# Batches 2 to 7 of a fused Fourier and ELU kernel in a schedule of 48 steps

## The chip, the core and the metric

The kernel runs on one core of a Trainium2 chip. The metric is the time of one execution on the device in microseconds (us). The kernel before takes 1938.01 us, the median of three runs (1937.81 to 1938.64). A measurement of this kernel can tell a difference of about 0.2% from none.

## The reference

Each of 8 batches of 3008 rows and 256 channels gets a two-dimensional Fourier transform, of which the real part is kept; the 24064 rows then go through two matrix products with an ELU between them.

```python
def _attn_ref(x):                     # x: (8, 3008, 256), float32
    X = np.fft.fft(x, axis=1)
    X = np.fft.fft(X, axis=2)
    return X.real.astype(np.float32)

def _moe_ref(x, w_in, w_out):         # x: (24064, 256), d_ff = 2048
    h = x @ w_in
    g = np.where(h > 0.0, h, np.exp(np.minimum(h, 0.0)) - 1.0)
    return (g @ w_out).astype(np.float32)
```

## The kernel before

**Folding.** The transform over channels is folded into the first weight matrix (Wc for cosines, Ws for sines), so what is left of the front is a transform over rows. Rows k and 3008-k of the result share their cosine and sine parts, P and Q: one gets P+Q, the other P-Q. So the kernel works on half of the frequencies, 1504 columns a batch, of which the first 752 are the even and the last 752 the odd frequencies (`kodd` 0 and 1).

**The main loop.** The 8 x 1504 columns are cut into 47 output tiles of 256. A tile takes 8 steps, one for each pair of feature blocks of 128, so there are 376 steps, and a batch is 47 steps long. In a step, with S as its number:

- `mm_P` starts the PSUM bank H with Wc times the cosine ring Rr, `mm_Q` adds Ws times the sine ring Ir (`first_mm`).
- VectorE adds the one cosine row that has no place in 128 rows (`even_part`, E, L1179) between the two, and after `mm_Q` makes the other half (`h_minus`, L1193).
- ScalarE makes Relu and Exp of both (`below_*`, `exp_*`), and in the next step VectorE finishes the ELU (`g_plus`, `g_minus`, L1209).
- GpSimd makes four sums of blocks of G (`sum_1` to `sum_4`), with which seven products do the work of eight (`mm_X1`, `mm_X2`, `mm_X3`, after Winograd); they add up in the banks pA to pD over the 8 steps of a tile.

A matmul in the code is two TensorE instructions in the trace, so a step has 22. When a tile is done, VectorE combines the banks (`comb_1`, `comb_2` in the step with number 1 modulo 8, `comb_22`, `comb_3` at 2), transposes (`turn_u` at 3, `turn_v` at 4) and SyncE stores it.

**The row transforms.** The rings Rr, Ir and Rb hold 2048 columns, so a batch's transforms are made while the batch before is in the loop. Batches 0 and 1 are made by the class `Dft`. For batches 2 to 7 the rows are loaded in quarters (`load_quarter`: four tiles xl0 to xl3, `far` 0 and then 1; each of the two loads has two plain DMAs and two gathers on GpSimd's queue). Then:

- `mirror_sum` on GpSimd adds mirrored rows, `half_sum` on VectorE adds or subtracts halves (two instructions of 256 elements), `channel_fold` on GpSimd and `channel_edge` on ScalarE fold the channels.
- `quarter_pairs` makes the last sums: for even frequencies on GpSimd, for odd ones on VectorE, as pairs of scalar_tensor_tensor with a table of tangents ("twisted pairs", L756).
- The class `Quarter` does the transform of each of four kinds (real or imaginary part `ri`, even or odd `kodd`), each in two halves. `mms` are eight TensorE instructions into a bank H; `copy`, `unfold`, `copy_odd` and `unfold_odd` turn banks into runs of columns, and `plus` and `minus` ("join") write both halves of the ring.

**The order.** It is written out by hand. Every piece of work is entered with a due time, `at(step * T + offset, function)` with T = 4.8, and emitted in order of these times; engine instructions made through `pin` keep that order on their engine, while plain SyncE DMAs aren't pinned. So each engine runs one fixed queue, and what is late in it makes all behind it late. In a step VectorE's queue has `even_part` at 0.9, the unfolding and joining at 1.0, `g_plus` at 2.2, `g_minus` at 2.9, `h_minus` at 3.55, and at 4.2 or 4.25 the tile's combining, the transposes, `half_sum` and the twisted pairs. GpSimd's folds stand at 1.3, between `sum_4` and the next `sum_1` (2.91). A transform's matmuls stand at 4.75, ahead of the next step.

For batch b the times are given from s0 = 47(b-1): the first loads at s0-12, the second ones at s0+7, the transforms at s0+28, s0+32, s0+36 and s0+42. As 47 is no multiple of 8, these lie in another place of the output tile for every batch. The function `pause` moves `half_sum` and the twisted pairs out of places 1, 3 and 4. `safe` is the first step at which a column of the ring may be written again.

Of the kernel before, what the change touches and what calls it, by code (L numbers as in the profile page):

```python
# [31 lines left out]
QW = (1133, 1134)  # L32
GW = 7 * TW
PERIOD = 4.8


def _dft_consts():
# [124 lines left out]
def kernel(  # L162
# [112 lines left out]
    def load_quarter(b, j, far):  # L275

        L = spool.tile([128, 6 * ND], FP, tag=f"xl{j}", bufs=1, name=f"xq{j}")
        state["L", j, far] = L = L[:, 0 : 4 * ND]
        back = j in (1, 2)
        base = (0, SEQ, HALF, HALF)[j]  # L280
        if back != far:
            n = 94 if far else 96
            c = 3 if far else 5 if j == 1 and b == NB - 1 else 4
            pin(
                nc.gpsimd.indirect_dma_start(
                    out=L[0:n],
                    out_offset=None,
                    in_=xflat,
                    in_offset=bass.IndirectOffsetOnAxis(
                        ap=ix[0:n, c : c + 1].bitcast(U32), axis=0  # L290
                    ),
                    element_offset=(b * SEQ + (HALF if j in (1, 3) else 0)) * ND,
                )
            )
            return
        row = base - 751 if far else base
        for p, q in ((0, 80), (80, 94)) if far else ((0, 96),):
            nc.sync.dma_start(out=L[p:q], in_=xrows(b, row + 8 * p, 8, q - p, 4))
# [430 lines left out]
                act(L[0:1, i * ND : i * ND + ND], L[0:1, i * ND + ND : i * ND + 2 * ND])  # L729
        act(L[0:1, 3 * ND :], state["L", 0, 0][0:1, 0:ND])  # L730

    def quarter_pairs(ri, kodd, m):
# [3 lines left out]
        if m == 1 + kodd:  # L736
            state["pairs"] = spool.tile([128, 384], FP, tag="side", bufs=2, name="pairs")
            state["Q", ri, kodd] = {0: near[0:95, 0:128], 4: slot(4)}
        new, parts = state["pairs"], state["Q", ri, kodd]
        for k in (m,) if kodd else (1, 2, 3):  # L740
            parts["u", k], parts["v", k] = new[0:94, 128 * k - 128 : 128 * k], slot(8 - k)
        if not kodd:
            a, b = (
                t[0:94, 128:512].rearrange("p (m d) -> p m d", d=128)
                for t in (near, far)
            )
            o = new[0:94].rearrange("p (m d) -> p m d", d=128)
            if m == 1:
                gtt(o, a, b[:, ::-1], ALU.add)
            else:  # L750
                gtt(b[:, ::-1], a, b[:, ::-1], ALU.subtract)
            return
        for i, o in ((0, parts["u", m]), (1, parts["v", m])):
            c = 4 * (0, 2, 1)[m - 1] + 2 * ri + i
            pin(
                nc.vector.scalar_tensor_tensor(  # L756
                    out=o, in0=parts["v", m], scalar=twist_tab[0:94, c : c + 1],
                    in1=slot(m), op0=ALU.mult, op1=ALU.add,
                )
            )  # L760
# [59 lines left out]
    class Dft:  # L820
# [18 lines left out]
            act(self.anti[0:M, 0:h], self.even[0:M, h : 2 * h])  # L839

        def unfold(self):
            self.es = spool.tile([128, NE], FP, tag="bs", bufs=3, name="bs")
            unfold(self.es, self.even, self.anti, self.M, self.n, vtt)

        def copy_odd(self):
# [43 lines left out]
    class Quarter(Dft):  # L889
# [50 lines left out]

        def unfold(self):
            M, ri, kodd = self.M, self.ri, self.kodd
            na, nc_ = (94, 188) if kodd else (95, 189)
            n = NO if kodd else NE
            self.es = es = spool.tile([128, NE], FP, tag="bs", bufs=3, name="bs")
            ab = spool.tile([128, 2 * NH], FP, tag="ab", bufs=1, name="ab")
            a, b = self.even[0:M, 0:na], self.near[0:M, 0:na]
            vtt(ab[0:M, 0:na], a, b, ALU.add)
            p, q = (b, a) if ri else (a, b)
            vtt(ab[0:M, steps_of(nc_ - 1, 94, -1)], p[:, 0:94], q[:, 0:94], ALU.subtract)  # L950
            if kodd:
                c = ab[:, NH : 2 * NH]
                self.spread(c, self.even[:, 94:189], self.near[:, 94:189], 94)
                runs = ((0, 1, 188, 188, c),)
            else:
                runs = (
                    (0, 2, 95, 94, self.even[:, 190:285]),
                    (1, 2, 94, 94, self.even[:, 285:379]),
                )
            for h, step, up, down, c in runs:  # L960
                i = steps_of(h, up, step)
                vtt(es[0:M, i], ab[0:M, i], c[0:M, 0:up], ALU.add)
                p, q = ab[0:M, steps_of(h, down, step)], c[0:M, 0:down]
# [9 lines left out]

        def unfold_odd(self):
            if self.kodd:
                t = spool.tile([128, NE], FP, tag="bs", bufs=3, name="od")
                self.spread(t, self.odd, self.far, 188)
                self.odd = t

# [119 lines left out]
    def ext_unfold(kodd, tt, rows=NB):  # L1099
        n = NO if kodd else NE  # L1100
        h = (n + 1) // 2
        even = state["side", 0]
        a = spool.tile([128, NE], FP, tag="bs", bufs=3, name="bs")
        unfold(a, even, even[:, h : 2 * h], rows, n, tt)
        state["es"] = a[0:rows]

# [621 lines left out]
    def at_half(step, d, par, col):  # L1728
# [6 lines left out]

        at(t + 4.75, run)
        if par:
            at(t + T + 0.9, lambda: d().copy_odd())
            at(t + T + 1.0, lambda: d().unfold_odd())
# [6 lines left out]
    def at_dft(step, gap, b, ri, kodd, stat):  # L1746
        box = []

        def d():
            if not box:  # L1750
                box.append((Quarter if b > 1 else Dft)(ri, b, kodd, stat()))
            return box[0]

        at_half(step, d, 0, 0)
# [28 lines left out]
    at(35 * T + 4.76, lambda: ext_side(3))  # L1783
    at(36 * T + 0.2, lambda: ext_unfold(1, vtt))
    at(36 * T + 1.5, lambda: ext_rows(1, vtt))
    at(34 * T + 4.3, quarter_table)
    at(34 * T, lambda: nc.sync.dma_start(out=twist_tab[0:96], in_=QT_dr.ap()))
    for n in range(4):
        at(
# [22 lines left out]
    for kodd, step in ((0, 37), (1, 40)):  # L1812
        at(step * T + 1.0, lambda kodd=kodd: spread_ext(1, kodd))

    for b in range(2, NB):
        s0 = (b - 1) * steps_b
        def pause(step):
            while step % 8 in (1, 3, 4):
                step += 1
            return step  # L1820

        for far, start in ((0, s0 - 12), (1, s0 + 7)):
            for j, n in ((0, 0), (1, 0), (3, 1), (2, 1)):
                gather = (j in (1, 2)) != far
                at(
                    (start + n) * T + (1.3 if gather else 0.2),
                    lambda b=b, j=j, far=far: load_quarter(b, j, far),
                )
            if not far:
                at((start + 2) * T + 3.0, lambda b=b: quarter_row(b))  # L1830
            work, sums, step = start + 3, {}, 0
            for n in range(8):
                h, m, j = n // 4, n // 2, (0, 3)[n % 2]
                at(work * T + 1.3, lambda j=j, far=far, m=m: mirror_sum(j, far, m))
                if n % 4 == 3:
                    step = max(work, step)
                    for kodd in range(2):
                        step = sums[h, kodd] = pause(step + 1)
                        at(
                            step * T + 4.25,  # L1840
                            lambda kodd=kodd, far=far, h=h: half_sum(kodd, far, h),
                        )
                work += 1
            for n in range(8):
                h, kodd, ri = n // 4, n // 2 % 2, n % 2
                work = max(work, sums[h, kodd] + 1)
                key = (ri, kodd, far, h)
                at(work * T + 1.3, lambda key=key: channel_fold(*key))
                if h and not ri:
                    at(  # L1850
                        work * T + 4.0,
                        lambda kodd=kodd, far=far: channel_edge(kodd, far),
                    )
                work += 1
            assert far or work <= s0 + 7
        for n in range(4):
            ri, m = divmod(n, 2)
            at((work + n) * T + 1.3, lambda ri=ri, m=m: quarter_pairs(ri, 0, 1 + m))
        step = 0
        for n in range(6):  # L1860
            ri, m = divmod(n, 3)
            step = pause(max(step + 1, s0 + (31, 35)[ri]))
            at(
                step * T + 4.25,
                lambda ri=ri, m=(2, 1, 3)[m]: quarter_pairs(ri, 1, m),
            )
        for ri, kodd, step in ((0, 0, 28), (1, 0, 32), (0, 1, 36), (1, 1, 42)):
            at_dft(
                s0 + step, 2, b, ri, kodd, lambda ri=ri, kodd=kodd: state["Q", ri, kodd]
            )  # L1870
# [52 lines left out]
```

## Time and profile before

| what | value |
|---|---|
| median of three runs | 1938.01 us |
| profiled execution | 1939.31 us |
| its span, first to last instruction | 1937.5 us |
| granted TensorE clock, mean | 0.999 |
| matmul instructions | 9008 |
| VectorE, ScalarE, GpSimd instructions | 2714, 1710, 1843 |
| DMA | 71.88 MB, mean 37 GB/s |

The profile comes from one execution, which took 1939.31 us; the span leaves out 1.8 us around it. Engines are named PE (TensorE's matmuls), PEld (its weight loads), DVE (VectorE), ACT (ScalarE), POOL (GpSimd) and SP (SyncE, which issues DMAs). In rows of the timeline, start and duration come first, then engine, source line, operation, what is written and read, shape and count, and in brackets the idle time before it with what ended it. Nearly all matmuls have line L536, GpSimd's sums L545 and VectorE's sums L542, since helpers record them; they are told apart by tiles. H<-Rr is `mm_P`, H<-Ir is `mm_Q`, H<-QM is a transform of batches 2 to 7. xq is a tile of loaded rows, bs and ab are tiles of the unfolding, od that of the odd half, e and o the tiles of the channel folds.

### The profile page before, as it was taken

To read this page: it belongs to the slowest core of one execution; us is meant where nothing else is said; L and a number is where in the kernel's file an instruction comes from. 1 tells how busy PE (TensorE), PEld (TensorE's weight loads), DVE (VectorE), ACT (ScalarE), POOL (GpSimd) and SP (SyncE) were. 2 spreads that over 40 slices of the span, in tenths; PEclk is the share of its full clock that TensorE was granted. 3 is DMA by queue.
4 is the path that set the end of the run, shared out by engine and by line. 5 is a ranking of instruction groups with operands and counts; after the bars stand their busy time and mean duration, and the time that the engine had idled before them with its cause. 6 is when DMAs were issued, how large, how long until landed. Compare 5 with 4: busy or idle time off the path is not lost.

```text
span 1937.5 us, 27618 instructions
## 1 busy us (share of the span) xinstructions
PE 1922.8 (99%) x9008; PEld 1651.0 (85%) x9008; DVE 1421.3 (73%) x2714; ACT 873.8 (45%) x1710; POOL 1352.6 (70%) x1843
## 2 busy tenths in 40 slices
PE   9999999999999999999999999999999999999999
PEld 6788788888888888888888888888888888888887
DVE  8876666777867687676776768777687777767666
ACT  5644444444444444444444444444444444444443
POOL 4788767775677767776677766777667775556555
PEclk9999999999999999999999999999999999999999
DMA  8145212011011120210111101011011110100101
GB/s 334 44 35 35 60 31 56 19 31 41 11 46 28 21 46 11 50 31 13 42 21 43 33 10 43 20 44 42 15 30 28 36 21 16 17 12 12 23 11 23
DMA packets 271072, 71.88 MB, mean 37 GB/s; under 512 B 256814, under 2 KB 257730, under 8 KB 270928
## 3 DMA queue, kind: packets, MB, share of 16 engines
q1 hardware_dynamic: 257296, 57.34, 14.8%
q0 software_dynamic: 11456, 12.52, 2.1%
q8 instruction: 71, 1.16, 0.2%
q14 instruction: 73, 0.60, 0.1%
q10 hardware_dynamic: 2176, 0.26, 0.1%
HBM read 45.20 MB, written 24.80 MB: 36 GB/s over the span
## 4 chain that ended last, share of the span: by engine, by line
PE 89%; DVE 6%; POOL 2%; DMA 1%; issue 1%; SPq 0%; ACT 0%; DVEq 0%; POOLq 0%
PE H L536 35%; PE pC L536 15%; PE pD L536 15%; PE pB L536 15%; PE pA L536 7%; DVE E L1179 2%; DVE G L1209 1%; PE M L536 1%; POOL G L545 1%; DMA out_dram<-ot 1%; POOL WT L545 1%; DVE G L1193 1%; SPq L1410 0%; DVE v L542 0%; DVE bs L542 0%
## 5 line engine op out<-in xcount | busy, mean ns | idle before, releaser
L545 POOL TENSOR_TENSOR G<-G 128x256 f32<-128x256 f32 x1440 | 1041.2, 732 | 528.6 <-DVE G L1209 405.4
L548 ACT ACTIVATE G<-H 128x512 f32<-128x512 f32 x376 | 224.5, 597 | 938.0 <-DVE G L1193 933.3
L1179 DVE SCALAR_TENSOR_TENSOR E<-Rb,wex,H 128x256 f32<-128x256 f32 x752 | 327.2, 476 | 420.1 <-PE H L536 412.9
L536 PE MATMUL H<-Ir,Ws 128*128 128x256 f32 x1504 | 390.8, 382 | 5.5 <-DVE E L1179 5.3
L536 PE MATMUL H<-Rr,Wc 128*128 128x256 f32 x1504 | 387.8, 380 | 0.8 <-DVE Ir L542 0.8
L536 PE MATMUL pC<-G,WT 128*128 128x256 f32 x1440 | 370.4, 380 | 0.0
L536 PEld LDWEIGHTS H<-Ir,Ws 128*128 128x128 f32 x1504 | 276.4, 189 | 62.9 <-DVE E L1179 19.9
L536 PEld LDWEIGHTS H<-Rr,Wc 128*128 128x128 f32 x1504 | 282.1, 190 | 43.7 <-issue 2.2
L536 PEld LDWEIGHTS pC<-G,WT 128*128 128x128 f32 x1440 | 274.2, 190 | 37.5
L1193 DVE SCALAR_TENSOR_TENSOR G<-E,H 128x512 f32<-128x512 f32 x376 | 256.7, 683 | 42.3 <-POOL G L545 10.3
L1209 DVE SCALAR_TENSOR_TENSOR G<-G,H 128x512 f32<-128x512 f32 x376 | 255.5, 679 | 33.0 <-ACT G L548 32.8
L1209 DVE SCALAR_TENSOR_TENSOR G<-M,G 128x512 f32<-128x512 f32 x376 | 256.4, 682 | 0.4 <-ACT M L548 0.4
L548 ACT ACTIVATE G<-G 128x512 f32<-128x512 f32 x376 | 233.3, 621 | 0.0
L536 PE MATMUL pB<-G,w 128*128 128x256 f32 x784 | 229.4, 379 | 0.0
L536 PE MATMUL pD<-G,w 128*128 128x256 f32 x784 | 229.2, 379 | 0.0
L536 PE MATMUL pA<-G,w 128*128 128x256 f32 x784 | 229.2, 379 | 0.0
L548 ACT ACTIVATE M<-G 128x512 f32<-128x512 f32 x376 | 224.2, 596 | 3.1 <-DVE G L1193 3.1
L548 ACT ACTIVATE M<-M 128x512 f32<-128x512 f32 x376 | 221.1, 588 | 0.1
L536 PE MATMUL pB<-G,WT 128*128 128x256 f32 x720 | 216.1, 382 | 2.8 <-POOL G L545 2.5
L536 PE MATMUL pD<-G,WT 128*128 128x256 f32 x720 | 215.0, 380 | 0.4 <-DVE v L542 0.4
L536 PEld LDWEIGHTS pD<-G,w 128*128 128x128 f32 x784 | 149.1, 190 | 20.3
L536 PEld LDWEIGHTS pA<-G,w 128*128 128x128 f32 x784 | 148.9, 190 | 20.5
(178 smaller groups left out, 1528.7 us busy)
## 6 DMA issues: line engine op xcount, KB each, us to landing
out_dram<-ot SPq DMA_DIRECT2D x496, 32.0 KB
xq<-in_x_dram SPq DMA_DIRECT2D x12, 384.0 KB
out_dram<-ot SPq DMA_DIRECT2D x256, 2.0 KB
xq<-in_x_dram SPq DMA_DIRECT2D x12, 320.0 KB
Rb<-r SPq DMA_DIRECT2D x10, 376.0 KB
raw<-in_moe_w_in_dram SPq DMA_DIRECT2D x7, 512.0 KB
MC<-dft_mats SPq DMA_DIRECT2D x3, 943.5 KB
xl<-in_x_dram SPq DMA_DIRECT2D x4, 512.0 KB
```

The source lines that it names most:

```text
L536: nc.tensor.matmul(out_, lhsT=lhsT, rhs=rhs, start=start, stop=stop, skip_group_check=True)
L545: pin(nc.gpsimd.tensor_tensor(out=o, in0=a, in1=b, op=op))
L548: pin(nc.scalar.activation(out=o, in_=i, func=func, **kw))
L1179: nc.vector.scalar_tensor_tensor(out=S.E[:, c], in0=Rb[:, cols(i)], scalar=wex[:, f : f + 1], in1=S.H[:, c], op0=ALU.mult, op1=ALU.add,)
L1193: nc.vector.scalar_tensor_tensor(out=two(S.G[:, 0:512])[:, :, ::-1], in0=two(S.E), scalar=2.0, in1=two(S.H), op0=ALU.mult, op1=ALU.subtract,)
L1209: nc.vector.scalar_tensor_tensor(out=o, in0=e, scalar=-1.0, in1=h, op0=ALU.add, op1=ALU.max)
```

## The change

- Batches 2 to 7 get a table of steps counted from r0 = 48b - 70, so that each piece stands at the same place in an output tile for all batches. Loads, sums, folds, pairs, transforms and joins all get new steps. For batch 2, whose r0 is 26, the first load moves from step 35 to 28; for batch 7 it moves from 270 to 268. The loop over batches remains 47 steps a batch.
- `Quarter` is entered by a function of its own, `at_quarter`. For odd frequencies `unfold` is parted: its last two instructions become `finish`, entered at offset 4.26 of a step of its own, and `plus` and `minus` move from the step of `unfold_odd` to offset 4.25 of a later step.
- The small tile "ab" goes; its work is done in the last third of the tile xl0 (`state["rest"]`), which the quarter loads leave free. Twisted pairs are written into the free last third of the fold tiles e and o instead of tiles "side".
- The tag "bs" has four buffers instead of three. The state of the pairs is kept for each batch.
- `quarter_table` (four small instructions on GpSimd) moves from step 34 to 27.

The core of the diff:

```diff
+BS = 4
...
         L = spool.tile([128, 6 * ND], FP, tag=f"xl{j}", bufs=1, name=f"xq{j}")
+        if j == 0:
+            state["rest"] = L[:, 4 * ND :]
...
+        new = (near, near, far)[m - 1][0:94, (512, 640, 512)[m - 1] :]
+        parts["u", m], parts["v", m] = new[:, 0:128], slot(8 - m)
...
         def unfold(self):
             M, ri, kodd = self.M, self.ri, self.kodd
-            na, nc_ = (94, 188) if kodd else (95, 189)
-            n = NO if kodd else NE
-            self.es = es = spool.tile([128, NE], FP, tag="bs", bufs=3, name="bs")
-            ab = spool.tile([128, 2 * NH], FP, tag="ab", bufs=1, name="ab")
+            na, top = (94, 187) if kodd else (95, 188)
+            self.ab = ab = state["rest"]
             a, b = self.even[0:M, 0:na], self.near[0:M, 0:na]
             vtt(ab[0:M, 0:na], a, b, ALU.add)
             p, q = (b, a) if ri else (a, b)
-            vtt(ab[0:M, steps_of(nc_ - 1, 94, -1)], p[:, 0:94], q[:, 0:94], ALU.subtract)
+            vtt(ab[0:M, steps_of(top, 94, -1)], p[:, 0:94], q[:, 0:94], ALU.subtract)
             if kodd:
-                c = ab[:, NH : 2 * NH]
+                c = ab[:, ND : ND + NH]
                 self.spread(c, self.even[:, 94:189], self.near[:, 94:189], 94)
-                runs = ((0, 1, 188, 188, c),)
+            else:
+                self.finish()
+
+        def finish(self):
+            M, ri, kodd, ab = self.M, self.ri, self.kodd, self.ab
+            n = NO if kodd else NE
+            self.es = es = spool.tile([128, NE], FP, tag="bs", bufs=BS, name="bs")
+            if kodd:
+                runs = ((0, 1, 188, 188, ab[:, ND : ND + NH]),)
             else:
...
-    at(34 * T + 4.3, quarter_table)
+    at(27 * T + 4.3, quarter_table)
...
+    def at_quarter(step, b, ri, kodd, finish, join):
...
+        at(step * T + 4.75, lambda: half(0))
+        at((step + 1) * T + 0.9, lambda: d().copy())
+        at((step + 1) * T + 1.0, lambda: d().unfold())
+        at((step + 2) * T + 4.75, lambda: half(1))
+        if kodd:
+            at(finish * T + 4.26, lambda: d().finish())
+            at((step + 3) * T + 0.9, lambda: d().copy_odd())
+            at((step + 3) * T + 1.0, lambda: d().unfold_odd())
+        assert join + 1 >= safe(b * HALF + (kodd + 1) * RUN)
+        t = join * T + (4.25 if kodd else 1.01)
+        at(t, lambda: d().plus())
+        at(t + 0.001, lambda: d().minus())
...
+        r0 = 48 * b - 70
+
+        def rel(step, dt, fn, *key):
+            at((r0 + step) * T + dt, lambda: fn(*key))
+
+        for far, rows in (
+            (0, ((0, 2, 0.2), (1, 2, 1.3), (3, 3, 0.2), (2, 3, 1.3))),
+            (1, ((0, 27, 1.3), (1, 25, 0.2), (3, 28, 1.3), (2, 27, 0.2))),
+        ):
+            for j, n, dt in rows:
+                rel(n, dt, load_quarter, b, j, far)
+        rel(5, 3.0, quarter_row, b)
+        for far, start in ((0, 6), (1, 30)):
             for n in range(8):
+                rel(start + n, 1.3, mirror_sum, (0, 3)[n % 2], far, n // 2)
+        for step, *key in (
+            (13, 0, 0, 0), (20, 1, 0, 0), (21, 0, 0, 1), (22, 1, 0, 1),
+            (35, 0, 1, 0), (36, 1, 1, 0), (37, 1, 1, 1), (38, 0, 1, 1),
+        ):
+            rel(step, 4.25, half_sum, *key)
+        for step, *key in (
+            (14, 0, 0, 0), (21, 1, 0, 0), (23, 0, 0, 1), (25, 1, 0, 1),
+            (38, 0, 1, 0), (40, 1, 1, 0), (42, 1, 1, 1), (44, 0, 1, 1),
+        ):
+            for ri in range(2):
+                rel(step + ri, 1.3, channel_fold, ri, *key)
...
         for n in range(4):
             ri, m = divmod(n, 2)
+            rel(46 + n, 1.3, quarter_pairs, b, ri, 0, 1 + m)
+        for n, step in enumerate((43, 44, 45, 46, 51, 53)):
             ri, m = divmod(n, 3)
+            rel(step, 4.25, quarter_pairs, b, ri, 1, (2, 1, 3)[m])
+        for step, ri, kodd, finish, join in (
+            (51, 0, 0, 0, 54),
+            (56, 1, 0, 0, 59),
+            (59, 0, 1, 60, 75),
+            (64, 1, 1, 66, 76),
+        ):
+            at_quarter(r0 + step, b, ri, kodd, r0 + finish, r0 + join)
```

More of the change, by code (lines that the diff above doesn't have):

```diff
@@ L730, in quarter_row, with quarter_pairs @@
         act(L[0:1, 3 * ND :], state["L", 0, 0][0:1, 0:ND])
-    def quarter_pairs(ri, kodd, m):
+    def quarter_pairs(b, ri, kodd, m):
         near, far = state["F", ri, kodd]
         slot = lambda m: (near, far)[m // 4][0:94, 128 * (m % 4) : 128 * (m % 4) + 128]
[L736 to L741, printed above, removed]
-        if not kodd:
-            a, b = (
+        parts = state.setdefault(("Q", ri, kodd, b), {0: near[0:95, 0:128], 4: slot(4)})
+        if not kodd:
+            if m == 1:
+                state["pairs"] = spool.tile(
+                    [128, 384], FP, tag="side", bufs=2, name="pairs"
+                )
+            new = state["pairs"]
+            a, z = (
                 t[0:94, 128:512].rearrange("p (m d) -> p m d", d=128)
@@ L748, in quarter_pairs @@
             if m == 1:
-                gtt(o, a, b[:, ::-1], ALU.add)
+                gtt(o, a, z[:, ::-1], ALU.add)
             else:
-                gtt(b[:, ::-1], a, b[:, ::-1], ALU.subtract)
+                gtt(z[:, ::-1], a, z[:, ::-1], ALU.subtract)
+            for k in (1, 2, 3):
+                parts["u", k] = new[0:94, 128 * k - 128 : 128 * k]
+                parts["v", k] = slot(8 - k)
             return
+        new = (near, near, far)[m - 1][0:94, (512, 640, 512)[m - 1] :]
+        parts["u", m], parts["v", m] = new[:, 0:128], slot(8 - m)
         for i, o in ((0, parts["u", m]), (1, parts["v", m])):
@@ L841, in unfold @@
         def unfold(self):
-            self.es = spool.tile([128, NE], FP, tag="bs", bufs=3, name="bs")
+            self.es = spool.tile([128, NE], FP, tag="bs", bufs=BS, name="bs")
             unfold(self.es, self.even, self.anti, self.M, self.n, vtt)
@@ L975, in unfold_odd @@
             if self.kodd:
-                t = spool.tile([128, NE], FP, tag="bs", bufs=3, name="od")
+                t = spool.tile([128, NE], FP, tag="bs", bufs=BS, name="od")
                 self.spread(t, self.odd, self.far, 188)
@@ L1102, in ext_unfold @@
         even = state["side", 0]
-        a = spool.tile([128, NE], FP, tag="bs", bufs=3, name="bs")
+        a = spool.tile([128, NE], FP, tag="bs", bufs=BS, name="bs")
         unfold(a, even, even[:, h : 2 * h], rows, n, tt)
@@ L1737, in at_half @@
         if par:
-            at(t + T + 0.9, lambda: d().copy_odd())
-            at(t + T + 1.0, lambda: d().unfold_odd())
             at(t + T + 1.01, lambda: d().plus())
@@ L1750, in d @@
             if not box:
-                box.append((Quarter if b > 1 else Dft)(ri, b, kodd, stat()))
+                box.append(Dft(ri, b, kodd, stat()))
             return box[0]
@@ L1813, with d, half @@
         at(step * T + 1.0, lambda kodd=kodd: spread_ext(1, kodd))
+    def at_quarter(step, b, ri, kodd, finish, join):
+        box = []
+        def d():
+            if not box:
+                box.append(Quarter(ri, b, kodd, state["Q", ri, kodd, b]))
+            return box[0]
+        def half(par):
+            d().ps = bank("H")
+            d().mms(par, d().ps)
+        at(step * T + 4.75, lambda: half(0))
[10 more added lines that the diff above has]
+        at(t + 0.001, lambda: d().minus())
@@ L1815 @@
     for b in range(2, NB):
         s0 = (b - 1) * steps_b
[L1817 to L1831, printed above, removed]
-            for n in range(8):
[L1833 to L1855, printed above, removed]
@@ new lines @@
+        for step, *key in (
[9 more added lines that the diff above has]
+                rel(step + ri, 1.3, channel_fold, ri, *key)
+            kodd, far, h = key
+            if h:
+                rel(step, 4.0, channel_edge, kodd, far)
@@ L1856 @@
         for n in range(4):
             ri, m = divmod(n, 2)
-            at((work + n) * T + 1.3, lambda ri=ri, m=m: quarter_pairs(ri, 0, 1 + m))
-        step = 0
-        for n in range(6):
+            rel(46 + n, 1.3, quarter_pairs, b, ri, 0, 1 + m)
+        for n, step in enumerate((43, 44, 45, 46, 51, 53)):
             ri, m = divmod(n, 3)
[L1862 to L1870, printed above, removed]
+            rel(step, 4.25, quarter_pairs, b, ri, 1, (2, 1, 3)[m])
[6 more added lines that the diff above has]
+            at_quarter(r0 + step, b, ri, kodd, r0 + finish, r0 + join)
```

## The prediction

> Words used below. A step is one pass of the main loop over a pair of feature blocks; its place is its number modulo 8, that is, where it stands in an output tile. s0 is 47(b-1) for batch b. In the changed kernel a relative step k is the step 48b-70+k; as 48 is a multiple of 8 and 70 is 72 less 2, its place is (k+2) modulo 8 for every b. Slot A is VectorE's time from h_minus (offset 3.55) to the next E, slot B the time just after E (offset 1.0).
>
> **What bounds the kernel now.** First the page:
>
> ```profile
> PE 1922.8 (99%) x9008; PEld 1651.0 (85%) x9008; DVE 1421.3 (73%) x2714; ACT 873.8 (45%) x1710; POOL 1352.6 (70%) x1843
> ...
> PE 89%; DVE 6%; POOL 2%; DMA 1%; issue 1%; SPq 0%; ACT 0%; DVEq 0%; POOLq 0%
> ```
>
> TensorE is the bound, but 99% hides what can be won: the chain of waits leaves it for VectorE in 6% and GpSimd in 2%. So I went to the timeline, first of an undisturbed step (start, duration, engine):
>
> ```profile
> 1286.63 1.03 PE L536 MATMUL H<-Rr,Wc 128*128 128x256 f32 x4
> ...
> 1287.70 0.87 DVE L1179 SCALAR_TENSOR_TENSOR E<-Rb,wex,H 128x256 f32<-128x256 f32 x2 [1.85 <-PE H L536]
> ...
> 1288.79 1.03 PE L536 MATMUL H<-Ir,Ws 128*128 128x256 f32 x4
> ...
> 1289.31 3.02 POOL L545 TENSOR_TENSOR G<-G 128x256 f32<-128x256 f32 x4 [1.04 <-DVE G L1209]
> ...
> 1291.38 1.03 PE L536 MATMUL H<-Rr,Wc 128*128 128x256 f32 x4
> ```
>
> From H<-Rr to H<-Rr is 4.75 us: 22 matmul instructions of 0.216 us from start to start. VectorE stands idle 1.85 us before E, and E's end (1288.57) is 0.2 us ahead of the matmuls that need it (1288.79), so slot A takes about 2.0 us of further work at no cost. GpSimd's four sums take 3.02 us and begin 1.04 us after it ran out of work.
>
> Then the timelines of VectorE and of TensorE where steps 274 and 275 (place 2, place 3) meet a transform of batch 6:
>
> ```profile
> 1425.16 0.60 DVE L542 TENSOR_TENSOR od<-H,far 128x188 f32<-128x188 f32 x2
> 1425.80 1.08 DVE L542 TENSOR_TENSOR Rr<-bs,od 128x376 f32<-128x376 f32 x3
> 1426.79 0.68 DVE L1209 SCALAR_TENSOR_TENSOR G<-G,H 128x512 f32<-128x512 f32 x1
> 1427.39 0.68 DVE L542 TENSOR_TENSOR v<-v,pD 128x512 f32<-128x512 f32 x1
> ...
> 1429.19 0.44 DVE L756 SCALAR_TENSOR_TENSOR pairs<-o,twist_tab,e 94x128 f32<-94x128 f32 x1
> 1429.66 0.77 DVE L756 SCALAR_TENSOR_TENSOR o<-o,twist_tab,e 94x128 f32<-94x128 f32 x1
> ```
>
> ```profile
> 1428.13 0.70 PE L536 MATMUL pD<-G,WT 128*128 128x256 f32 x2 [0.24 <-DVE v L542]
> ...
> 1430.34 0.70 PE L536 MATMUL pB<-G,WT 128*128 128x256 f32 x2 [0.22 <-POOL G L545]
> 1431.27 1.13 PE L536 MATMUL H<-Ir,Ws 128*128 128x256 f32 x4 [0.23 <-DVE E L1179]
> ```
>
> Unfolding and join (1.6 us, slot B), the tile's comb_3 and the twisted pairs (1.2 us, slot A) fall into two neighbouring steps; VectorE is late, g_plus is late, so GpSimd's sums are late, and TensorE stops three times: against 0.216 us a start, the stops and the first instruction after each cost 1.5 us in this step. The list of waits of the weight loads, over 393 to 1738 us (total, times, longest), says that this is the rule:
>
> ```profile
> PEld H L536 <- DVE E L1179: 15.9, 37, 0.8
> PEld pB L536 <- POOL G L545: 8.0, 16, 1.1
> ```
>
> **How much is there.** Steps 48 to 335 hold batches 2 to 7. Their first matmuls start at 293.9 and, for step 336, at 1732.3: 1438.4 us. Undisturbed: 288 x 22 x 0.216 = 1368.6; and 24 transforms of two halves, 0.86 us (1443.46 to 1444.32) and 1.28 us (1421.69 to 1422.97), 24 x 2.14 = 51.4. Sum 1420.0, so 18.4 us are lost. Counting each start more than 25 ns above its form's median gives 19.2 us at 134 places; 17.5 of them lie in s0+29 to s0+46, where transforms and twisted pairs are, 7.8 at place 3 and 4.2 at place 2, where the tile's own combining and transposes are. 24 of the 134 are the 30 ns after a transform (0.7 us), which stay.
>
> **What the Trainium skill says.** "Perfetto Trace Analysis", section "Identifying the Most-Contended Engine": matmul occupancy is no measure of the distance to the limit. Agreed: 99%, with 18.4 us lost. "SBUF — State Buffer", "Who interferes with whom": a VectorE instruction with two SBUF inputs and a GpSimd one that reads SBUF shut each other out. Agreed: half_sum (xq<-xq,xq, both inputs in SBUF) takes 0.48 to 0.49 or 0.93 to 0.95 us, by how GpSimd's sums lie. "TensorE: Matmul & The Clock Gate", "What's actually happening": activity sets whether the clock runs at full or half rate. Agreed: from 228.3 to 231.7 us, after two pauses in step 36, the granted clock is 0.50 and eight matmuls start 0.21 us later than usual, 1.7 us in all.
>
> **The change part by part.** Numbers of TensorE's and ScalarE's instructions don't change; what is won is stalls.
>
> Half sums (two instructions, 1.36 us) move to relative steps 13, 20 to 22 and 35 to 38, twisted pairs (0.44 + 0.77 us) to 43 to 46, 51, 53: places 5, 6, 7, 0, each alone in its slot A. 1.4 against 2.0 us: no cost. Two half sums in following steps stood so before (steps 109, 110), without a stall.
>
> Even transforms: unfold (six instructions, 1.2 us) in slot B of relative 52 and 57, join (five, 1.2 us) in 54 and 59; places 6, 3, 0, 5. Only place 3 has more, the transpose (0.70 us): 1.9 us in all, and before, step 123 had exactly this and lost 0.03.
>
> Odd transforms: what was six plus four instructions in two slots B is parted. Slot B of 60 and 65: four of 0.25 us; slot A of 60 and 66: finish, two of 0.35; slot B of 62 and 67: two of 0.35; slot A of 75 and 76: plus and minus, two of 0.55. Slot B never holds over 1.2 us now. Here is the one new pairing: finish and join read two SBUF operands and now run beside GpSimd's sums (0.73 us each), which in slot B they mostly didn't. No row shows that. Below: 0.55 and 1.0 us, nothing lost. Above: each instruction waits for a sum, 2 x 0.73 more: 2.0 and 2.5 us. Half_sum in the same slot comes to 1.36 us for two of 256 elements, one wait in two. So I take one: 1.3 for finish, 1.75 for join, under 2.0; but at 60, slot B's four are in the same step, and I put 0.2 us a batch there: 1.2 us.
>
> GpSimd: one fold (0.84), mirror sum (0.72), gather (0.92 to 1.49) or pair operation (1.00) a step, as before, at offset 1.3, where 1.7 us are free. Batch 2 alone meets batch 1: mirror sums in steps 32 to 38 beside batch 1's folds (1.0 us): 3.02 + 1.0 + 0.72 = 4.74 in a step of 4.75, 4.96 where the short extra sum (0.21) comes too. Sums may come about 1.4 us late before TensorE waits (sum_2 ends at about 4.9, its matmuls start 1.7 into the next step), transforms in 36 and 38 lengthen steps, and the four iotas (0.12 each) and two gathers leave steps 34 to 36: no cost. On VectorE, half sums now fall on 39 and 47 after joins of batch 1 (slot B 1.1, A 1.4, 2.5 in all); step 48 lost 0.19 us so before. I put 0.5 us for 39 and 48 together.
>
> DMAs: the plain loads sit in SyncE's queue, which isn't bound to the order of the code (the first one of batch 2, coded for step 35, was issued at 161.9 us); being ten steps sooner only frees them. Stores of a tile stand ahead of them for 4 to 7.4 us. Gathers are bound: the far ones land 10.3 to 12.2 us after issue and have three steps, 14.2 us, before and after. One mirror sum waited 3.3 us for a load (578 us), which cost TensorE 0.95; I keep half of that, 0.5. Results come in time: odd columns are needed from step 112 (batch 2) and 352 (batch 7) and are joined in 101, 102 and 341, 342; even ones from 88 and 328, joined by 85 and 325.
>
> The fourth "bs" buffer, the dropped "ab" tile, the pairs in the free ends of the fold tiles: no instruction more, no cost.
>
> **The sum.** 18.4 - 0.7 - 1.2 - 0.5 - 0.5 = 15.5 us. The profiled execution took 1939.3 (span 1937.5); 1939.3 - 15.5 = 1923.8. The median, 1938.0, is 1.3 below it, so 1922.5.
>
> **Rivals.** (1) The shared reads cost their upper end: finish at 60 and both joins come 0.4 us late, with 0.1 for the reload seen after every stop, 3 x 6 x 0.5 = 9 us instead of 1.2: 1930. For it: half_sum's 0.95. Against: the pairs in slot A, also two SBUF operands, stayed at 1.2 us for two.
>
> (2) The lost time only moves: VectorE's work is the same 1002 us of 1345, and at 75% a queue in fixed order can stall anywhere; three quarters of it come back: 1938.0 - 4 = 1934. Against: stretches with one item a step (101 to 104, 107 to 114) show no stall.
>
> (3) Slower: unfolding now writes in the last third of the tile into which, two steps earlier (relative 50), the next batch's first rows are loaded. If waits went by whole tiles, the first unfold (12.6 us after step 50 begins: 2 x 4.75, a half transform 1.28, 1.85) would wait for the landing. With stores ahead for 4.9 us (the transpose ends 0.7 us into that step; its eight stores take 4.2, as at 225.0) and a landing as slow as the slowest gather, 12.2, that is 17.1: 4.5 us, plus 1.7 for a spell at half clock, in five batches 31, less 15.5: 1953. It decides from a wait of 1.4 us on (15.5/5 - 1.7). Against: the ring Rb is one tile that DMAs refill while E reads other columns, and E's waits name no DMA.
>
> **Numbers.** Forecast 0.66, rival 1 0.17, rival 2 0.09, rival 3 0.08. This kernel's measurement tells 0.2%, 3.9 us, from no change: under 1934.1 is faster. Faster 0.66 + 0.17 = 0.83; rival 2 is at the edge and counts 0.08 as same, its last 0.01 as slower: slower 0.09. If all stalls go, and the spell at half clock (1.7) and step 36's shorter GpSimd wait with it, 1918; rival 1 reaches 1931: that leaves out 0.17 and a little at the ends.
>
> **What would show it.** The waits of H<-Ir for E and pB for GpSimd's G over these steps should fall from 24 us to under 4 in the weight loads; steps at places 2 and 3 should last 3.88 and 5.61 us (what they last undisturbed, by the late matmuls of place 2) apart from transforms; VectorE's and GpSimd's busy times stay within 1%. Wrong it would be if new rows with Rr<-bs,od or bs<-ab end waits of TensorE, if a VectorE row waits for a DMA into xq, or if steps 28 to 48 grow by more than 1 us.

## The result, and the profile after

The changed kernel takes 1926.43 us, the median of five runs (1925.81 to 1928.59), against 1938.01 before: ratio 0.9943, 95% interval 0.9929 to 0.9958. That is 11.6 us less; the forecast was 1922.5. (This ratio and those below are taken from the runs together, so they differ a little from the quotients of the medians.) Its profiled execution took 1925.81 us, with a span of 1924.0.

First the page of the changed kernel, busy times and chain:

```profile
PE 1910.7 (99%) x9008; PEld 1653.7 (86%) x9008; DVE 1436.7 (75%) x2714; ACT 872.7 (45%) x1710; POOL 1357.3 (71%) x1843
...
PE 86%; DMA 4%; POOL 3%; SPq 2%; DVE 2%; issue 1%; ACT 0%; POOLq 0%; DVEq 0%
```

VectorE's share of the chain fell from 6% to 2%. TensorE's own did not rise, from 89% to 86%: DMAs and SyncE's queue (SPq) now have 6% together, where they had 1%. The chain runs back through stretches in which a load waits behind stores. The line numbers have moved by 3 in the helpers and by 14 in the loop.

The waits of the weight loads over the same stretch of time as before, 393 to 1738 us (total, times, longest):

```profile
PEld pB L539 <- POOL G L548: 6.3, 5, 2.2
PEld H L539 <- issue: 1.4, 3, 0.8
PEld H L539 <- DVE E L1193: 1.2, 4, 0.4
```

Before, H<-Ir waited for E 37 times, 15.9 us in all; now it does so 4 times, 1.2 us. The waits of pB for GpSimd's sums went from 16 to 5, but these are up to 2.2 us long.

From the first matmul of step 48 to that of step 336 it takes 1426.1 us (before 1438.4). Less the matmuls' own time, 6.2 us are lost there where 18.4 were. Counted start by start, as in the prediction, it is 7.0 us at 41 places in place of 19.2 at 134. A further 1.1 of the 13.5 us by which the span shrank lies ahead of step 48; it comes up below.

Next VectorE's timeline in step 275 of the changed kernel (place 3), the later of the two steps that were shown for the kernel before, up to E of step 276. A transform of batch 6 is unfolded here too:

```profile
1413.82 0.87 DVE L1193 SCALAR_TENSOR_TENSOR E<-Rb,wex,H 128x256 f32<-128x256 f32 x2 [1.19 <-PE H L539]
1414.60 0.25 DVE L545 TENSOR_TENSOR xq<-H,near 127x95 f32<-127x95 f32 x1
...
1415.55 0.25 DVE L545 TENSOR_TENSOR bs<-H,xq 127x94 f32<-127x94 f32 x1
1415.71 0.68 DVE L1223 SCALAR_TENSOR_TENSOR G<-G,H 128x512 f32<-128x512 f32 x1
...
1417.51 0.70 DVE L1371 STREAM_TRANSPOSE ot<-u 128x512 f32<-128x512 f32 x1
1419.43 0.87 DVE L1193 SCALAR_TENSOR_TENSOR E<-Rb,wex,H 128x256 f32<-128x256 f32 x2 [1.21 <-PE H L539]
```

Slot B holds the six instructions of an unfolding, slot A the transpose, and VectorE still stands idle 1.2 us ahead of either E. TensorE takes 4.75 us for step 274 and 5.64 for step 275, which is without a stop.

What is left shows in the changed kernel's timelines of SyncE's queue, GpSimd and TensorE, over 541 to 582 us (in the rows of the queue, SPq, the second number is the time from the first to the last of the instructions joined in the row):

```profile
541.49 9.03 SPq L301 DMA_DIRECT2D xq<-in_x_dram  x3
550.63 24.95 SPq L1424 DMA_DIRECT2D out_dram<-ot  x40
575.63 0.33 SPq L301 DMA_DIRECT2D xq<-in_x_dram  x1
```

```profile
577.73 0.90 POOL L548 TENSOR_TENSOR xq<-xq,xq 94x255 f32<-94x255 f32 x2 [4.40 <-DMA xq<-in_x_dram]
```

```profile
580.85 0.70 PE L539 MATMUL pB<-G,WT 128*128 128x256 f32 x2 [1.83 <-POOL G L548]
```

A far load is four pieces, two tiles of 80 and 14 rows each. Three are issued, then 40 stores that take 25 us, and only then the last piece of 14 rows. The mirror sum needs it at relative step 31. GpSimd waits for it (2.9 to 4.4 us in batches 3 to 7), the four sums behind it come late, and TensorE stops. The changed kernel does this at steps 106, 154, 202, 250 and 298, exactly 48 apart: 2.10, 1.19, 0.61, 0.87 and 0.87 us, 5.6 of the 7.0. In batch 2, where 32 stores stand ahead of the last piece, GpSimd waits 0.27 us and TensorE doesn't stop. In the kernel before, the far load of batch 3 was cut in this way (at 546, 555 and 579 us). In the next four batches all four pieces went ahead of the 40 stores, as here in its SyncE queue:

```profile
780.21 11.05 SPq L298 DMA_DIRECT2D xq<-in_x_dram  x4
...
792.89 24.34 SPq L1410 DMA_DIRECT2D out_dram<-ot  x40
```

### The profile page after: what moved, and what is told of

Read it like the earlier page. It is cut to its first block, busy times and chain, and to the rows that moved or that the text cites. A ratio compares the mean times of both kernels' runs of the same rounds, so it can differ in the third digit from the quotient of the medians.

```text
span 1924.0 us, 27630 instructions
## 1 busy us (share of the span) xinstructions
PE 1910.7 (99%) x9008; PEld 1653.7 (86%) x9008; DVE 1436.7 (75%) x2714; ACT 872.7 (45%) x1710; POOL 1357.3 (71%) x1843
## 3 DMA queue, kind: packets, MB, share of 16 engines
q1 hardware_dynamic: 257296, 57.34, 15.1%
## 4 chain that ended last, share of the span: by engine, by line
PE 86%; DMA 4%; POOL 3%; SPq 2%; DVE 2%; issue 1%; ACT 0%; POOLq 0%; DVEq 0%
PE H L539 34%; PE pB L539 15%; PE pC L539 15%; PE pD L539 15%; PE pA L539 7%; DMA out_dram<-ot 4%; SPq L1424 2%; POOL G L548 2%; POOL WT L548 1%; DMA xq<-in_x_dram 1%; DVE G L1223 0%; DMA xl<-in_x_dram,ix 0%; POOL e L548 0%; DVE E L1193 0%; DVE e L636 0%
```

## The experiments

There were two theories. One: the fixed place gives the gain, because VectorE's extra work no longer meets the tile's combining and transposes; what remains is the one late load. The rival: the parting of the unfolding and the earlier start give it, and the place is of no matter. Each time below is the median of 4 to 13 executions. The ratio is to the kernel before as it ran beside that kernel: 1938.28 us for the first four experiments and 1938.81 for the last four. "Lost" is the excess over the matmuls' own time in steps 48 to 335, from one profile each and good to about 0.1 us.

| kernel | median us | ratio to before, 95% interval | lost us |
|---|---|---|---|
| changed | 1926.43 | 0.9943 (0.9929 to 0.9958) | 6.2 |
| other order of far sums | 1920.58 | 0.9906 (0.9891 to 0.9921) | 0.6 |
| far loads whole | 1920.81 | 0.9907 (0.9892 to 0.9922) | 0.6 |
| unbound | 1945.02 | 1.0035 (1.0021 to 1.0048) | 23.4 |
| unparted | 1927.83 | 0.9945 (0.9932 to 0.9959) | 6.6 |
| before, bound | 1934.55 | 0.9978 (0.9970 to 0.9986) | 15.1 |
| unbound, order and finish moved | 1938.56 | 1.0000 (0.9992 to 1.0008) | 17.1 |
| order, unparted | 1922.14 | 0.9916 (0.9902 to 0.9930) | 2.4 |
| order, two places later | 1956.21 | 1.0091 (1.0077 to 1.0105) | 35.6 |

**The late load, by the order of the sums.**

```diff
-                rel(start + n, 1.3, mirror_sum, (0, 3)[n % 2], far, n // 2)
+                j, m = ((0, 3)[n // 2 % 2], n // 4 * 2 + n % 2) if far else ((0, 3)[n % 2], n // 2)
+                rel(start + n, 1.3, mirror_sum, j, far, m)
```

> The changed kernel, but the far mirror sums take the two tiles in the order 0, 0, 3, 3, 0, 0, 3, 3, so that the first sum over the late-loaded pair of tiles comes one step (4.75 us) later. Theory (fixed place freed VectorE; what is left, 5.65 of 7.0 us in steps 48 to 335, is GpSimd waiting 2.9 to 4.4 us for the last piece of the far load, in every batch at relative step 31): the wait shrinks under 0.5 us, the five stops of pB<-G,WT for GpSimd go, about 5.6 us less: 1920.8. Rival (the stops come from GpSimd's own load in that step, not from the wait): the stops stay or move one step on, within 1 us of the changed kernel, 1926.

1920.58 us. The five stops are gone. The chain of waits and the waits of the weight loads (393 to 1738 us) of this kernel:

```profile
PE 96%; DVE 1%; POOL 1%; ACT 0%; issue 0%; DMA 0%; DVEq 0%; POOLq 0%
```

```profile
PEld H L539 <- issue: 1.7, 4, 0.8
PEld H L539 <- DVE E L1193: 0.9, 3, 0.4
```

DMA and SPq have left the chain, and no row of pB for GpSimd is among the waits. The load is no sooner: its last piece is still issued behind the 40 stores, at 574.9 us. The sum that needs it is one step later. All 24 steps at place 2 that hold no transform now last 3.88 us, and all 36 at place 3 between 5.61 and 5.64; in the kernel before the longest were 4.83 and 7.10.

**The late load, by whole loads.**

```diff
-        for p, q in ((0, 80), (80, 94)) if far else ((0, 96),):
+        for p, q in ((0, 94),) if far else ((0, 96),):
```

> The changed kernel, but each far plain load is one transfer of 94 rows in place of two of 80 and 14. Theory (the last of four pieces is issued after 40 stores, 24 us late, because of its place in SyncE's queue): with two pieces in place of four none is left behind the stores, GpSimd's wait goes, 5.6 us less: 1920.8. Rival (a whole load is just as late behind the stores, or a transfer of 94 rows lands later): GpSimd's wait is as long or longer, 1926 or more, up to 1932 if the whole 94 rows are late for the sums.

1920.81 us, with nothing else altered. SyncE's queue in the timeline of this kernel:

```profile
542.16 9.00 SPq L301 DMA_DIRECT2D xq<-in_x_dram  x2
551.26 28.12 SPq L1424 DMA_DIRECT2D out_dram<-ot  x40
```

Both loads now go ahead of the stores. Two different edits, one of the need and one of the supply, give back the same 5.6 to 5.9 us, so the cause of these stops is shown: the last piece comes too late for the sum at step 31.

**The place taken away.**

```diff
-        r0 = 48 * b - 70
+        r0 = 47 * b - 68
```

> The changed kernel with its whole table of steps, parting and earlier folds, but counted from 47b - 68 in place of 48b - 70: the same start for batch 2, and then each batch one place earlier in the output tile. Theory (the gain comes from the fixed place): VectorE's transforms and pairs meet the tile's combining and transposes again in batches 3 to 7, stops of H<-Ir for E and of pB for GpSimd's G come back at places 2 and 3, 8 to 12 us more than the changed kernel: 1934 to 1938. Rival (the parting of the unfolding and the earlier folds bring the gain): within 2 us of the changed kernel, 1924 to 1928.

1945.02 us, worse than expected and worse than before. Its waits of the weight loads for E over 393 to 1738 us:

```profile
PEld H L539 <- DVE E L1193: 26.8, 37, 2.0
```

The rival falls: the same pieces, parted and early, lose 23.4 us once they drift. But the loss has two sources. At 47 steps a batch, step 60 of one batch meets step 13 of the next, so finish and a half sum share a slot A, which has nothing to do with the place in a tile. The steps after this meeting (87, 134, 181, 228 and 275) lost 1.0 to 1.9 us each, 7.3 in all. (The 8.2 in an expectation below counts step 322 too; it belongs to batch 7, which meets no next one.) The next kernel but two takes the meeting out.

**The parting undone.**

```diff
-            else:
-                self.finish()
+            self.finish()
...
-            at(finish * T + 4.26, lambda: d().finish())
...
-        assert join + 1 >= safe(b * HALF + (kodd + 1) * RUN)
-        t = join * T + (4.25 if kodd else 1.01)
+        assert step + 4 >= safe(b * HALF + (kodd + 1) * RUN)
+        t = (step + 3) * T + 1.01
```

> The changed kernel in its fixed places, but the odd transforms are not parted: their last two unfolding instructions follow the first four at once, and plus and minus follow unfold_odd in its step, as before. Theory (fixed place is enough; slot B of these steps has room for 1.5 to 1.6 us): 0 to 1 us more than the changed kernel, 1926.4 to 1927.4, since the two steps have no other work for VectorE but the transposes' neighbours. Rival (the parting is what frees TensorE): g_plus comes late in 24 steps with 0.3 to 0.5 us of stop each, 5 us more or above: 1931 or more.

1927.83 us, 1.4 more than the changed kernel: neither theory's number. Its waits of the weight loads for GpSimd over 393 to 1738 us:

```profile
PEld pB L539 <- POOL G L548: 8.7, 17, 1.4
```

Twelve of the 17 stops are new, one step after each whole join, 0.15 to 0.23 us each and 2.1 in all; two stops of the joins in slot A, 0.4, are gone. The late load cost 4.3 us here and 5.6 in the changed kernel, so a small difference had to be taken again without it.

**The kernel before in a fixed place.**

```diff
-        s0 = (b - 1) * steps_b
+        own = (b - 1) * steps_b
+        s0 = 48 * b - 46
...
-            step = s0 + (28, 38)[kodd]
+            step = own + (28, 38)[kodd]
```

> The kernel before with its own table of steps, unparted and with its own fold times, but counted from 48b - 46 in place of 47(b-1), so that every batch has the places that its batch 7 has. Theory (a fixed place helps only with work laid into the free places): the losses by batch of before lie between 1.7 (batch 7's stretch, without loads for a next batch) and 3.9 us; six times 1.7 to 3 make 10 to 18 us in place of 18.4: 1930 to 1938. Rival (not drifting is what counts, whatever the places): close to the changed kernel, 1922 to 1927.

1934.55 us: 4.3 less than the kernel before beside it, inside the range expected. Steps 48 to 335 lose 15.1 us. Its waits of the weight loads over 393 to 1738 us:

```profile
PEld H L536 <- DVE E L1179: 18.1, 40, 1.1
PEld pB L536 <- POOL G L545: 3.8, 14, 0.4
```

E is waited for as often as before, now at the same steps in every batch (places 2, 6 and 0). With the old table and in this one phase, not drifting is worth little more than a third of what the change brings, and the rival misses by 7 us or more.

**Drift alone.** The unbound kernel again, with the order of sums from the first experiment, and:

```diff
-            (59, 0, 1, 60, 75),
+            (59, 0, 1, 61, 75),
```

> The changed kernel counted from 47b - 68 again, now with the sums in the order 0, 0, 3, 3 and with the first finish at step 61 in place of 60, since at 47 steps a batch it met the next batch's half sum of step 13 (60 - 47) in one slot A, which cost 8.2 of the 23.4 us lost. Theory (drift against the output tile costs by itself): the other 15 us stay, 14 to 15 more than the 1920.6 of the kernel with only that order changed: 1933 to 1937. Rival (the loss of the unbound table was this one meeting between batches): 1921 to 1925.

1938.56 us, 18.0 more than the kernel with only the order changed, and no faster than before. It is 6.5 us faster than the unbound kernel, and 6.3 of these lie in the five steps after a meeting and in step 322. Of the 18.0, 16.5 lie in steps 48 to 335, and 1.5 in step 338 (place 2), behind a join of batch 7. The losses grow with the drift: 0.2 us in steps 48 to 94, 6.3 in steps 236 to 282, where batch 6 is four places off, and 5.8 in the 47 steps after. Its waits:

```profile
PEld H L539 <- DVE E L1193: 20.5, 34, 1.6
```

Six stops make 7.8 of the 17.1 us (steps 250, 258, 282, 290, 298 and 306). Each stands in a step at place 2, behind a half sum, a twisted pair or a join that the drift has put into slot A of the step before, at place 1. So the table that does best in its own places does no better than the old one out of them. The old one kept its half sums and twisted pairs off places 1, 3 and 4 by `pause`, which the new table doesn't call.

**Parting, without the late load.** The edits of the first and the fourth experiment together.

> The changed kernel with the sums in the order 0, 0, 3, 3 (no wait for the late load) and the odd transforms not parted. Theory (parting only removes the twelve stops of pB of 0.15 to 0.23 us, 2.1 in all, that the unparted kernel showed one step after the whole unfolding and after the join, and pays 0.4 for its own joins): 1.7 more than 1920.6, 1922.3. Rival (those stops came from GpSimd being late through the load): 1920 to 1921. Rival (parting carries most of the gain): 1927 or more.

1922.14 us, 1.6 above the parted one: as the theory had it. Times alone can't tell so small a difference (the intervals in the table overlap). The twelve stops do: they stand at the same steps as in the unparted kernel and make 2.1 us again, and steps 48 to 335 lose 1.8 us more than in the parted kernel. The rows of the step after a whole join, in the timeline of this kernel:

```profile
495.67 3.04 POOL L548 TENSOR_TENSOR G<-G 128x256 f32<-128x256 f32 x4 [3.49 <-DVE G L1222]
...
497.95 0.30 PEld L539 LDWEIGHTS pB<-G,WT 128*128 128x128 f32 x2 [0.36 <-POOL G L548]
```

In slot B, the second half of the unfolding and the join hold VectorE for 1.6 us (493.21 to 494.84). g_plus comes so much later, GpSimd stands idle 3.5 us (2.6 at the same place in the parted kernel), and its sums miss TensorE by a little.

**The same table two places later.** The first experiment's order, and:

```diff
-        r0 = 48 * b - 70
+        r0 = 48 * b - 68
```

> The changed kernel with the sums in the order 0, 0, 3, 3, still 48 steps a batch, but counted from 48b - 68: every piece two places later in the output tile, so half sums and pairs (steps 13, 20 to 22, 35 to 38, 43 to 46) fall on places 0, 1, 2 and 7 in place of 5, 6, 7 and 0. Theory (the choice of the places makes the gain): a half sum at place 2 beside comb_3 cost 1.3 us in the unbound kernel; two of these a batch, 0.5 for the pairs at place 2 and some 0.1 for each of four pieces at place 1 make 3.5 a batch, 21 in all: 1941. Rival (any fixed place will do): 1920.6 to 1924.

1956.21 us: 15 more than the theory's figure, and the slowest of all. The stops in steps 50 and 66 cost 1.59 and 1.58 us and that in step 74 costs 1.48, and so on every 48 steps: 27.9 us, all at place 2. Another 2.7 are the late load, which came back in three batches, since the pieces now stand otherwise to the stores; 3.0 of the rest stand at place 3, in the step after an even join.

But the expectation had its prices at the wrong place. Step 50 in this kernel's timeline:

```profile
302.94 0.68 DVE L545 TENSOR_TENSOR u<-p,pB 128x512 f32<-128x512 f32 x1
...
303.46 1.03 PE L539 MATMUL H<-Rr,Wc 128*128 128x256 f32 x4
...
303.72 0.69 DVE L545 TENSOR_TENSOR v<-u,pC 128x512 f32<-128x512 f32 x1
304.33 1.94 DVE L545 TENSOR_TENSOR xq<-xq,xq 96x256 f32<-96x256 f32 x2
306.19 0.86 DVE L1193 SCALAR_TENSOR_TENSOR E<-Rb,wex,H 128x256 f32<-128x256 f32 x2
...
307.10 1.13 PE L539 MATMUL H<-Ir,Ws 128*128 128x256 f32 x4 [1.32 <-DVE E L1193]
...
309.69 1.44 DVE L545 TENSOR_TENSOR xq<-xq,xq 96x256 f32<-96x256 f32 x2
```

The half sum that stops step 50 is the one of relative step 21. It was entered at step 49, place 1, and stands behind comb_1 and comb_2: 3.3 us of work in a slot A of about 2.0. In the same way the stops in steps 66 and 74 stand behind the half sum and the pair of steps 65 and 73, also place 1, which the expectation put at 0.1 us each. The half sum of step 50 itself (the last row, at place 2), which it put at 1.3, cost 0.10 us, though VectorE was late from the stop before; that of step 66 cost as much, and the pair of step 74 nothing. In the unbound kernel, too, the half sum that stood alone in the slot A of a place 2 (step 202) cost only 0.05. (The other pieces at place 1, relative steps 13 and 53, stand ahead of half a transform in batches 2 to 7, but for step 13 of batch 2; they stop nothing, and that one costs 0.94 us in step 42.)

The changed kernel's timeline shows why place 1 is dear. It lays nothing there, and still slot A is full (steps 105 and 106):

```profile
576.61 0.68 DVE L545 TENSOR_TENSOR u<-p,pB 128x512 f32<-128x512 f32 x1
577.39 0.69 DVE L545 TENSOR_TENSOR v<-u,pC 128x512 f32<-128x512 f32 x1
578.19 0.87 DVE L1193 SCALAR_TENSOR_TENSOR E<-Rb,wex,H 128x256 f32<-128x256 f32 x2
```

E starts 0.1 us after comb_2 ends, and that is when it is due: 4.75 us after the E before it, which had 1.85 us of idle time ahead.

## Why the prediction was right, and where it missed

Direction and mechanism held: 0.57% is more than the 0.2% that can be told, 1926.43 lies in the range of 1918 to 1931, and the unbound kernels and the one two places off show that the gain is one of place. The gain itself was forecast 3.9 us too large, and one term alone was out by 5.1; the small terms, out the other way, hid part of that by luck. By its steps:

- **Half sums, pairs and even transforms: no cost.** Right. None of them stops TensorE in batches 3 to 7; the two stops in batch 2 come under steps 39 and 48.
- **Odd transforms, finish at 60: 1.2 us, with shared reads.** The reads are shared, and it cost next to nothing. Groups of VectorE's instructions by shape, over 393 to 1738 us (count, busy us, mean ns), in the changed kernel and then in the one unparted with the other order:

```profile
L545 DVE TENSOR_TENSOR bs<-xq 128x188 f32<-128x188 f32 x12 | 8.8, 769 | 0.0
...
L545 DVE TENSOR_TENSOR Rr<-bs,od 128x376 f32<-128x376 f32 x8 | 6.0, 783 | 0.0
...
L545 DVE TENSOR_TENSOR Ir<-bs,od 127x376 f32<-127x376 f32 x4 | 3.7, 929 | 0.0
```

```profile
L545 DVE TENSOR_TENSOR Rr<-bs,od 128x376 f32<-128x376 f32 x10 | 5.1, 547 | 0.2
...
L545 DVE TENSOR_TENSOR bs<-xq 128x188 f32<-128x188 f32 x12 | 3.7, 351 | 0.2
...
L545 DVE TENSOR_TENSOR Ir<-bs,od 127x376 f32<-127x376 f32 x5 | 2.7, 550 | 0.2
```

  Out of slot B and beside GpSimd's sums, one instruction of finish takes 769 in place of 351 ns, one of a real join 783 in place of 547 and one of an imaginary join 929 in place of 550. The Trainium skill's page "SBUF — State Buffer", section "Who interferes with whom", says that a VectorE instruction with two SBUF inputs contends with a GpSimd one that reads SBUF; these times agree with it. Two of them make 1.5 us for finish, 1.7 for a real join and about 2.0 for an imaginary one (batches 3 to 5). That is nearer to the 1.3 and 1.75 put down than to the upper end of 2.0 and 2.5, and it fits into a slot A of about 2.0. In batch 6 the columns cross the end of the ring, so a join is three instructions, 2.2 and 2.4 us; these alone cost something, 0.4 us (steps 294 and 295), but for 0.03 in step 103. Rival 1 had the mechanism right and its size wrong.
- **Parting.** The prediction gave it no figure of its own. It is worth 1.6 us (1922.14 against 1920.58), or 1.8 by the time of steps 48 to 335.
- **Steps 39 and 48: 0.5 us.** 0.19 in step 48, and 0.25 in step 40, after the half sum in 39: right.
- **DMAs: one load's wait kept half, 0.5 us.** This is the step that failed. It cost 5.6 us. The wait at 578 us had been seen and priced, but taken as a chance event that may come or not. In a schedule that repeats every 48 steps a meeting of load and stores isn't one chance: it stopped TensorE in five batches here, and in three in the kernel two places later. The sentence that being sooner only frees the loads looked at when a load may start, not at what would stand ahead of its last piece. And stores were said to stand ahead of a load for 4 to 7.4 us, while the same trace has 32 of them for 21.5 us (from 312.95) and 40 for 23.8 us (from 555.38) between the pieces of a far load. Had the sum taken 5.6 for 0.5, it would have kept 10.4 us of gain in these steps, where 12.3 were found. The rest is small: finish and joins cost 0.4 and not 1.2, step 48 alone 0.2 and not 0.5, and the losses kept were counted start by start, as the 19.2 are, but taken from the 18.4.
- **The sum.** Steps 48 to 335 gained 12.3 us, not 15.5. The profile's span gained 1.1 more ahead of step 48. That is mostly the spell at half clock near 228 us (1.7 us), which the trace of before has and that of after hasn't; a new 0.25 in step 40 and 0.2 at the start of step 36 go the other way. The spell doesn't seem to be a gain of the change: without it the two spans would lie 11.8 us apart, and the medians lie 11.6 apart. Both kernels have some slower executions, two of nine at 1940.1 and 1940.5 us before and two of five at 1928.6 now; that these hold such a spell is likely and not shown, as they were not profiled.
- **Rival 2, lost time only moves.** Refuted for VectorE (E's waits went from 15.9 to 1.2 us). What stayed is mostly another engine's wait, at one point in a batch, and it has a cause of its own.
- **Rival 3, unfolding waits for a landing in xl0.** Refuted: no row of VectorE names a DMA into xq, and the unfolding above runs without a gap.
- **What would show it.** Waits of 24 us were to fall under 4: they fell to 7.5 (6.3 of them the late load) and with the order changed to 0.9. Steps at place 3 last 5.61 to 5.64; at place 2, 19 of the 24 without a transform last 3.88, and the other five hold the late load. GpSimd's busy time rose by 0.3%, VectorE's by 1.1%, just over the 1% named. With the odd transforms unparted and the other order it is 1421.8 us against 1421.3 before. Against that kernel, finish and joins take 19.6 us more in the changed one and half sums 3.0 less, so the rise is the shared reads.

Open: what starting the folds ten steps sooner brings by itself, since the table leaves no room to put them back at the same places; and what the old table would do in another fixed phase. The fourth "bs" buffer, the dropped tile "ab" and the new place of the pairs are in all kernels made from the changed one, and their part wasn't taken alone.

## What to carry to other kernels

Where two periodic patterns share engines, first make one period a multiple of the other (here 48 steps and 8), and then choose the phase. The old table with the first alone gave 4 us; the new table lost 17 in one phase and gained 18 in another, with one order of the far sums in both. A schedule bound in this way repeats its accidents: a wait seen a single time in the drifting kernel is to be priced both at zero and at the number of periods, and one looks at what stands ahead of it in its queue, DMA issues included. Room in a fixed queue is not the same at every place, so it is read from the timeline place by place: here about 2.0 us in an undisturbed step, and at place 1 about 0.3 (0.1 us of idle time, and the 0.2 by which E is early). And the piece to blame for a stop is the one ahead of it in the queue, which can have been entered a step earlier.

## What the runs showed of the hardware

- A VectorE add of two SBUF operands that falls beside GpSimd's sums lost 0.2 to 0.4 us in the mean, the shorter ones no less than the longer: 188 elements went from 351 to 769 ns (finish), 376 elements from 550 to 929 (the imaginary join; the real one from 547 to 783).
- 40 stores in a row, issued after a far load, held SyncE's queue for 18 to 31 us (23 to 25 in the changed kernel, about 0.6 us for each). A load of 14 rows that is issued behind them is late by all of that, and one transfer of 94 rows in place of 80 and 14 cost the kernel nothing (1920.81 against 1920.58 us).
- A stop of TensorE costs about 0.1 us beyond the wait itself in nearly all of the stops counted here: the first start after it comes 0.104 us late. Twelve stops of 0.04 to 0.13 us so made 2.1 us.
